# High and low parts of a short last row group side by side in one stationary block

## The chip, the cores and the metric

The kernel runs on one core of one Trainium2 chip. The metric is the time of one execution on the device in microseconds (us). The core has five engines that run at the same time and wait for each other through semaphores: TensorE (PE in the profile, its weight loads PEld), VectorE (DVE), ScalarE (ACT), GpSimd (POOL) and SyncE (SP), which here issues loads. Sixteen DMA engines move data.

## The reference

Windowed attention makes 8 x 544 = 4352 rows of 512 values. Each row goes to one of eight experts, and the expert's two layers are applied to it. Which expert a row gets is known only once the attention is done.

```
logits = einsum('bsd,de->bse', x, w_gate)
local_gate = 1 / (1 + exp(-einsum('bsd,de->bse', x, w_local)))
for b in range(8):
    for s in range(544):
        fresh = argmax(logits[b, s])
        e = fresh if s == 0 or local_gate[b, s] < 0.5 else prev_e
        prev_e = e
        p = softmax(logits[b, s])
        h = maximum(x[b, s] @ w1[e], 0)          # 512 -> 1024
        out[b, s] = p[e] * (h @ w2[e])           # 1024 -> 512
```

## The kernel before

The first third of the time is attention. Routing then makes, on the chip, lists of the rows of each expert. The rest is the expert part, class `Moe`, which works in blocks. An early block and a full block take 256 rows of an expert. Each expert also has one remainder block, called e0 to e7 below, which takes what is left over after its blocks of 256 and, where the expert has a block of 256 that no other block took, those 256 rows as well. Rows stand in groups of 128, numbered 0 to 3: in a remainder block with a block of 256, groups 0 and 1 are those 256 rows, and groups 2 and 3 the remainder.

Products are made to full precision from two roundings each: a value is the sum of a high part and a low part, and a product of two values is three products, high by high, high by low and low by high. The weights come in eight pieces of 512 KB for a block, four for each layer; `load` issues one on SyncE, `split` rounds it to its high part on ScalarE (L1150) and subtracts on VectorE for its low part (L1160).

A remainder block runs like this:

- `block` reads the case number of the expert, which routing wrote into `cnd`, and enters one of 34 copies of the code with `Switch`. Case 0 is `half`, a remainder of at most 128 rows with no block of 256. Case 2 and up are `part` with 256 rows and a remainder of 8, 16, ... 256 rows. All five engines jump into the case and out of it at its end.
- `mm1`, first layer: for each of eight slices `fc` of 128 hidden values, 12 products (L1251) with the weights stationary and the rows as columns, so the width of a product is the number of rows. ScalarE takes the positive part as high part into `HH` (L1253), VectorE the low part into `HL` (L1254). The eight slices rotate through five banks of PSUM, `ps` 2, 3, 6, 1, 7.
- `mm2`, second layer: for each row group, for each slice, three products of 128x512 (L1262) in which the rows' high or low parts are the stationary block of 128 x 128 and the weights' parts stream past. That is 24 products for a group, into one bank.
- `store` scales a group's result by each row's probability (ScalarE, L1267) and scatters the rows to the output (GpSimd, L1268).
- `xpose` transposes one row group of the next block on TensorE (L1205), and ScalarE and VectorE copy its parts (L1207, L1208). Groups 0 and 1 are transposed in the case, after 9 and 18 second-layer products; groups 2 and 3 in `close`.
- `close` stands behind the case and is the same code for all cases of an expert: it stores the group that the case left in `ps[7]`, makes the 24 products of group 2, works out the scales of the next block (`scals`, L1217 to L1219, the first VectorE work after a case) and gathers the rows of the block after it (`gather`, GpSimd, L1191).

In the order of row groups, a remainder over 128 ran `[3, 0, 1]` and then 2 in `close`; a smaller one `[0, 1]` and then 2.

Two generators do the routing in small steps, hidden behind the early blocks: `Moe.hook` runs after each slice of an early block and takes one step of them. `Route.lists` writes the numbers of the row groups that each block gathers into `cid`, compares them with each row's number, and multiplies one-hot tables on TensorE (L999, 34 products) to get the rows' indices; two of its steps are taken per hook. `kinds` makes the case numbers, three steps per hook, and `rest` the indices of all later blocks, two per hook. In the middle of the second layer of the last early block `finish` runs what is missing up to the case numbers, at once.

## Time and profile before

| | us |
|---|---|
| median of 3 runs | 699.48 |
| lowest and highest run | 695.32, 699.75 |
| the profiled execution, its time | 698.19 |
| the profiled execution, its span | 696.5 |

The span runs from the first to the last instruction of the profiled execution; 1.7 us lie around it. The mean granted clock of TensorE was 0.990. Attention ends near 240 us, the early blocks run to 326 us, the remainder blocks to 619 us, three full blocks to 688 us.

Lines of a timeline have the start in us, the duration of the run of instructions, the engine, the source line, the operation, its output and inputs by name, the shapes, and the number of instructions; in brackets, how long the engine was idle before it and what ended the wait. Durations of matmuls overlap, so the pace of a run is read from starts, or from the chain of waits, where a row has the start, the time that it adds to the chain, and the number of instructions.

### The profile page before, as it was taken

What the parts mean: (1) busy time and instruction counts of PE and PEld (TensorE: products, weight loads), DVE (VectorE), ACT (ScalarE), POOL (GpSimd) and SP (SyncE); (2) the same over time, 40 slices, a digit from 0 to 9 for tenths busy, and PEclk for the clock granted to TensorE, in tenths of its full rate; (3) what the DMA queues carried; (4) which work ended last, traced back from release to release, by engine and by line L of the source; (5) the groups of instructions that cost most, each with busy time, mean ns of one, the idle gap of its engine ahead of it and who ended that gap; (6) DMA issues with size and microseconds to landing.
All of it is one profiled execution on the core that took longest, in us unless ns stands there. A gap on an engine that the chain in (4) does not pass through costs nothing.

```text
span 696.5 us, 18391 instructions
## 1 busy us (share of the span) xinstructions
PE 671.7 (96%) x7253; PEld 564.2 (81%) x7253; DVE 427.4 (61%) x1057; ACT 342.6 (49%) x614; POOL 196.2 (28%) x321
## 2 busy tenths in 40 slices
PE   9999999999899899998997999999999999999995
PEld 7777777777677787897886898889898989888994
DVE  7878777678887777995516645426353516345563
ACT  4555555655454674652326535334444425255563
POOL 7634344243333301032013303031304021032033
PEclk9999999999999999999999999999999999999998
DMA  8956967866846497776517666428385417265673
GB/s 331 387 213 238 353 235 274 311 240 226 309 181 262 140 353 247 257 230 238 191 60 257 200 219 200 145 76 257 126 260 158 159 66 235 67 211 179 234 259 112
DMA packets 43014, 151.46 MB, mean 217 GB/s; under 512 B 7965, under 2 KB 9245, under 8 KB 38688
## 3 DMA queue, kind: packets, MB, share of 16 engines
q1 hardware_dynamic: 35536, 126.92, 51.5%
q0 software_dynamic: 6960, 21.90, 9.8%
q8 instruction: 77, 1.26, 0.7%
q14 instruction: 153, 1.25, 0.5%
q10 hardware_dynamic: 288, 0.13, 0.1%
HBM read 130.55 MB, written 19.69 MB: 216 GB/s over the span
## 4 chain that ended last, share of the span: by engine, by line
PE 59%; DVE 3%; issue 1%; ACT 1%; POOL 0%; DVEq 0%; ACTq 0%; POOLq 0%
PE ps L1262 28%; PE ps L1251 26%; PE ps L1205 3%; DVE wp L1160 1%; DVE wq L1160 1%; PE ps L1374 0%; DVE xT L991 0%; PE ps L999 0%; POOL xa L1191 0%; DVE xT L989 0%; DVE hl L1254 0%; DVE wp L1208 0%; PE ps L276 0%; PE ps L1363 0%; DVE xl L1160 0%
## 5 line engine op out<-in xcount | busy, mean ns | idle before, releaser
L1268 POOL DMA_INDIRECT out_dram<-y,tk x39 | 40.5, 1039 | 320.0 <-ACT y L1267 257.0
L1262 PE MATMUL ps<-wp,wq 128*128 128x512 f32 x504 | 128.0, 401 | 0.9 <-ACT wq L1365 0.9
L1262 PEld LDWEIGHTS ps<-wp,wq 128*128 128x128 f32 x504 | 93.2, 190 | 20.5 <-ACT wq L1365 1.1
L1251 PE MATMUL ps<-wp,wp 128*128 128x256 f32 (+6 forms) x672 | 107.8, 320 | 0.0
L1251 PEld LDWEIGHTS ps<-wp,wp 128*128 128x128 f32 x672 | 103.4, 189 | 3.6
L1254 DVE SCALAR_TENSOR_TENSOR wq<-ps,wq 128x256 fp32r<-128x256 f32 (+6 forms) x80 | 41.3, 519 | 71.8 <-ACT wq L1253 71.6
L191 POOL TENSOR_SCALAR_AFFINE_SELECT qbd<-raw 64x512 f32<-64x512 f32 x62 | 44.6, 719 | 119.5 <-PE ps L243 100.6
L1208 DVE TENSOR_TENSOR wp<-ps,wp 128x512 fp32r<-128x512 f32 x40 | 27.4, 690 | 80.0 <-ACT wp L1207 80.0
L1253 ACT ACTIVATE wq<-ps 128x256 fp32r<-128x256 f32 (+6 forms) x80 | 36.8, 463 | 77.3 <-PE ps L1251 69.6
L243 PE MATMUL ps<-kx,qbd 128*64 128x128 f32 x1024 | 71.4, 281 | 1.8 <-issue 1.7
L243 PEld LDWEIGHTS ps<-kx,qbd 128*64 128x64 f32 x1024 | 55.1, 137 | 12.7 <-issue 8.3
L1267 ACT ACTIVATE y<-ps,pp 128x512 f32<-128x512 f32 x39 | 26.9, 689 | 76.4 <-PE ps L1262 70.8
L248 DVE TENSOR_REDUCE mx<-ps 128x4 f32<-128x512 f32 x64 | 43.9, 686 | 29.3 <-PE ps L243 29.3
L1160 DVE TENSOR_TENSOR wp<-raw,wp 128x1024 fp32r<-128x1024 f32 x47 | 56.9, 1216 | 2.5 <-ACT wp L1150 2.5
L254 ACT ACTIVATE pe<-pe 128x512 f32<-128x512 f32 x64 | 40.7, 636 | 32.9 <-DVE pe L250 32.9
L1191 POOL DMA_INDIRECT xa<-xs,idx x42 | 51.3, 1220 | 17.1 <-issue 10.0
L1150 ACT CAST wp<-raw 128x1024 fp32r<-128x1024 f32 x49 | 50.7, 1045 | 1.3 <-DMA raw<-in_w_dram 0.5
L1207 ACT CAST wp<-ps 128x512 fp32r<-128x512 f32 x40 | 23.4, 588 | 55.4 <-PE ps L1205 55.4
L250 DVE TENSOR_TENSOR pe<-ps,mx 128x512 f32<-128x512 f32 x64 | 44.0, 688 | 1.6
L276 PE MATMUL ps<-v,pt 128*32 128x65 f32 x2048 | 42.7, 222 | 2.1 <-DVE xa L284 0.8
L276 PEld LDWEIGHTS ps<-v,pt 128*32 128x32 f32 x2048 | 33.3, 110 | 13.8 <-issue 6.7
L191 POOL TENSOR_SCALAR_AFFINE_SELECT kx<-raw 128x384 f32<-128x384 f32 (+3 forms) x127 | 42.7, 369 | 3.0 <-DMA raw<-in_qk_dram 0.9
(279 smaller groups left out, 1173.0 us busy)
## 6 DMA issues: line engine op xcount, KB each, us to landing
raw<-in_w_dram SPq DMA_DIRECT2D x78, 512.0 KB, 3.9
v<-in_vw_dram SPq DMA_DIRECT2D x32, 1040.0 KB, 9.9
raw<-in_qk_dram SPq DMA_DIRECT2D x32, 528.0 KB, 8.2
xa<-in_w_dram SPq DMA_DIRECT2D x26, 512.0 KB, 5.0
xT<-in_w_dram SPq DMA_DIRECT2D x20, 512.0 KB, 4.1
xs<-xa SPq DMA_DIRECT2D x8, 1056.0 KB
qgb<-in_qg_dram SPq DMA_DIRECT2D x8, 128.0 KB
xa<-xs,idx POOLq DMA_INDIRECT x42
```

The source lines that it names most:

```text
L191: self.nc.gpsimd.affine_select(out=out, in_=in_, pattern=pat, compare_op=ALU.is_ge, fill=0.0, base=0, channel_multiplier=0)
L243: nc.tensor.matmul(sp[64 * t2:64 * t2 + 64, t], qbd[:, w], kf[:, f:f + P], start=False, stop=True, skip_group_check=True)
L248: nc.vector.tensor_reduce(out=mx, in_=st["sp"], axis=AX.X, op=ALU.max)
L250: nc.vector.tensor_tensor(out=st["pe"][:, 4 * hb:4 * hb + 4], in0=st["sp"], in1=mx.broadcast_to([P, 4, P]), op=ALU.subtract)
L254: self.nc.scalar.activation(out=pe, in_=pe, func=AF.Exp, scale=SCALE)
L276: nc.tensor.matmul(o[32 * w4:32 * w4 + 32, g, h], pt[:, 2 * g + w4 // 2, w4 % 2, h, :], v[:, w, h * (D + 1):(h + 1) * (D + 1)], start=True ...
L1150: nc.scalar.copy(out=hi, in_=raw)
L1160: (nc.gpsimd if pool else nc.vector).tensor_tensor(out=lo, in0=raw, in1=hi.bitcast(F32), op=ALU.subtract)
L1191: self.nc.gpsimd.indirect_dma_start(out=self.xr[j] if k == "early" else self.xr4[:, j], out_offset=None, in_=src, in_offset=bass.IndirectO ...
L1251: nc.tensor.matmul(ph, a[:, dc, fs], b_[:, dc, n0:n1], start=(n == 0), stop=(n == 11))
L1254: nc.vector.scalar_tensor_tensor(out=hl[:, fc, n0:n1], in0=ph, scalar=0.0, in1=hh[:, fc, n0:n1].bitcast(F32), op0=ALU.max, op1=ALU.subtract)
L1262: nc.tensor.matmul(py, a[:, fc, js], b_[:, fs], start=(fc == 0 and k == 0), stop=(fc == 7 and k == 2))
```

## The change

In a remainder block whose last row group has at most 64 rows (`HALF`), the low parts of the first layer's values of that group are no longer written to `HL`. They go into `HH`, into the columns 64 to 127 of group 3, beside the high parts in columns 0 to 63. The second layer of that group, `thin`, then takes two products for a slice, the block by the weights' high part and by their low part, 16 in place of 24. In its result the partitions 0 to 63 hold what the high parts gave and 64 to 127 what the low parts gave (with low by low, which was left out before), for the same rows. `store` adds the two: ScalarE scales the lower half into `y`, VectorE scales the upper half and adds.

For this the last group is always group 3. With a remainder of at most 128 rows the block of 256 moves from groups 0 and 1 to 1 and 2, and the first layer reads columns 128 to 384 + `few` in place of 0 to 256 + `few`. Routing takes that into account: `lists` shifts the numbers of the row groups by one for such experts, with six small instructions in place of two and four yields more. The order of groups in the case is `[0, 3, 1]` over 128; up to 128 it is the first half of the slices of group 1, then group 3, then the second half of group 1. `close` is unchanged, and so is the number of gathers.

```diff
-        cr = cid[:, 0:2 * E].rearrange("p (e a) j -> p e a j", a=2)
+        cr = cid[:, 0:2 * E].rearrange("p (e a) j -> p e (a j)", a=2)
-        nc.vector.tensor_scalar(out=cr[:, :, 0, 0], in0=self.nbc, scalar1=-4.0, scalar2=None, op0=ALU.add)
-        yield
-        nc.vector.tensor_scalar(out=cr[:, :, 1, 0], in0=self.nbc, scalar1=-2.0, scalar2=None, op0=ALU.add)
+        rm = self.tmp("rm", [P, E], I32)
+        nc.vector.tensor_scalar(out=rm, in0=self.cn, scalar1=255, scalar2=None, op0=ALU.bitwise_and)
+        yield
+        sh = self.tmp("sh", [P, E], F32)
+        nc.vector.tensor_scalar(out=sh, in0=self.left, scalar1=0.0, scalar2=None, op0=ALU.is_ge)
+        yield
+        nc.vector.scalar_tensor_tensor(out=sh, in0=rm, scalar=float(P), in1=sh, op0=ALU.is_le, op1=ALU.mult)
+        yield
+        fb = self.tmp("fb", [P, E], F32)
+        nc.vector.scalar_tensor_tensor(out=fb, in0=self.nbc, scalar=-4.0, in1=sh, op0=ALU.add, op1=ALU.subtract)
+        yield
+        nc.vector.tensor_tensor(out=cr, in0=fb.rearrange("p (e o) -> p e o", o=1).broadcast_to([P, E, 4]),
+                                in1=self.io8[:, 0:4].rearrange("p (o j) -> p o j", o=1).broadcast_to([P, E, 4]), op=ALU.add)
+        yield
+        nc.vector.scalar_tensor_tensor(out=cr[:, :, 0], in0=sh, scalar=4.0, in1=fb, op0=ALU.mult, op1=ALU.add)
         yield
...
-        nc.vector.scalar_tensor_tensor(out=hl[:, fc, n0:n1], in0=ph, scalar=0.0, in1=hh[:, fc, n0:n1].bitcast(F32), op0=ALU.max, op1=ALU.subtract)
+        for o, a, b_ in [(hl, n0, n1)] if not few else [(hl, n0, n1 - few), (hh, n1 - few, n1)]:
+            c = a if o is hl else P * (NSL - 1) + HALF
+            nc.vector.scalar_tensor_tensor(out=o[:, fc, c:c + b_ - a], in0=ph[:, a - n0:b_ - n0], scalar=0.0, in1=hh[:, fc, a:b_].bitcast(F32), op0=ALU.max, op1=ALU.subtract)
...
+    def thin(self, i, py, fc, j, hh):
+        hi, lo = self.wp[8 * i + 4 + fc // 2]
+        fs = slice(512 * (fc % 2), 512 * (fc % 2) + 512)
+        for k, b_ in enumerate((hi, lo)):
+            self.nc.tensor.matmul(py, hh[:, fc, P * j:P * j + P], b_[:, fs], start=(fc == 0 and k == 0), stop=(fc == 7 and k == 1))
...
+        if thin:
+            nc.scalar.activation(out=y[rows], in_=py[HALF:P], func=AF.Copy, scale=g[HALF:P, js])
+            nc.vector.scalar_tensor_tensor(out=y[rows], in0=py[rows], scalar=g[rows, js], in1=y[rows], op0=ALU.mult, op1=ALU.add)
...
+        thin = 0 < few <= HALF
+        if thin:
+            g = self.g[0]
+            self.nc.vector.tensor_copy(g[HALF:P, 3:4], g[0:HALF, 3:4])
...
-            n = 256 + GRAIN * (case - 1)
-            self.part(i, 0, n, [3] * (n > 384) + [0, 1])
+            few = GRAIN * (case - 1)
+            if few <= P:
+                self.part(i, P, 384 + few, [(1, range(4)), (3, range(8)), (1, range(4, 8))], few)
+            else:
+                self.part(i, 0, 256 + few, [(0, range(8)), (3, range(8)), (1, range(8))], few - P)
```

On TensorE, in the case of e3 with 184 remainder rows (last group 56), this stood where the group in the middle of the three is worked out. A row is a source line, the operation, output and inputs with buffer numbers, the shape and a count; `ps_64` is the bank, `wq_4314` is `HH`, `wq_4315` is `HL`, the `wp` are pieces of weights. Before, group 0 stood there, of which these are the first half:

```order
L1262 MATMUL ps_64<-wp_101,wq_4314 128x512 x2
L1262 MATMUL ps_64<-wp_101,wq_4315 128x512
L1262 MATMUL ps_64<-wp_101,wq_4314 128x512 x2
L1262 MATMUL ps_64<-wp_101,wq_4315 128x512
L1262 MATMUL ps_64<-wp_4207,wq_4314 128x512 x2
L1262 MATMUL ps_64<-wp_4207,wq_4315 128x512
L1262 MATMUL ps_64<-wp_4207,wq_4314 128x512 x2
L1262 MATMUL ps_64<-wp_4207,wq_4315 128x512
```

After, in the same place, group 3, with the first rows of group 1 behind it:

```order
L1284 MATMUL ps_64<-wp_101,wq_4314 128x512 x4
L1284 MATMUL ps_64<-wp_4207,wq_4314 128x512 x4
L1284 MATMUL ps_64<-wp_4208,wq_4314 128x512 x4
L1284 MATMUL ps_64<-wp_4312,wq_4314 128x512 x4
L1278 MATMUL ps_70<-wp_101,wq_4314 128x512 x2
```

Group 3 moved from the front to the middle, reads only `HH`, and has 16 products.

On VectorE, in the routing behind the second early block, the two instructions that wrote `cid` stood here before (`nbc` counts groups, `wp` rows split a piece of weights):

```order
L1254 SCALAR_TENSOR_TENSOR hl<-ps_66,hh 128x256
L1011 TENSOR_SCALAR cid<-nbc 128x8
L1013 TENSOR_SCALAR cid<-nbc 128x8
L1017 TENSOR_TENSOR mf<-ge,sd 128x104
L1020 SCALAR_TENSOR_TENSOR k_4713<-ek,k_269 128x13
L1160 TENSOR_TENSOR wp_4311<-xa_108,wp_4311 128x1024
```

After, `rm` is the remainder, `sh` tells whether an expert's groups are shifted, `fb` is the first group's number:

```order
L1270 SCALAR_TENSOR_TENSOR hl<-ps_66,hh 128x256
L1014 TENSOR_SCALAR rm<-cn 128x8
L1017 TENSOR_SCALAR sh<-left 128x8
L1019 SCALAR_TENSOR_TENSOR sh<-rm,sh 128x8
L1022 SCALAR_TENSOR_TENSOR fb<-nbc,sh 128x8
L1174 TENSOR_TENSOR wp_4311<-xa_108,wp_4311 128x1024
L1024 TENSOR_TENSOR cid<-fb,io_262 128x32
L1027 SCALAR_TENSOR_TENSOR cid<-sh,fb 128x8
```

`mf` and all routing steps after it stand two hooks later than before.

On ScalarE, at the end of the case of e5 with 32 remainder rows, the copies of the next block's transposed groups 0 and 1 (`wp_4209`, from the banks 68 and 67) stood together, with the store of group 0 (`y_4318`, from bank 63) as the last work before the jump:

```order
L1253 ACTIVATE wq_4314<-ps_69 128x288
L1207 CAST wp_4209<-ps_68 128x4x128
L1207 CAST wp_4209<-ps_67 128x4x128
L1267 ACTIVATE y_4318<-ps_63,pp_94 128x512
L1566 UNCONDITIONAL_BRANCH
```

After:

```order
L1267 ACTIVATE wq_4314<-ps_69 128x288
L1221 CAST wp_4209<-ps_68 128x4x128
L1293 ACTIVATE y_4318<-ps_64,pp_94 64x512
L1221 CAST wp_4209<-ps_67 128x4x128
L1608 UNCONDITIONAL_BRANCH
```

The store is that of group 3, covers 64 partitions and comes ahead of the second copy. That copy now comes behind the sixth slice of group 1 and is the last work before the jump.

More of the change, by code (lines that the diff above doesn't have):

```diff
@@ L49 @@
 REM = 2
+NSL = 4
+HALF = P // 2
 NPIECE = 12
@@ L1393, in part @@
                 self.nc.gpsimd.drain()
[L1394 removed]
+            self.mm1(i, fc, *x, n0, n1, self.ps[(2, 3, 6, 1, 7, 2, 3, 6)[fc]], few if thin else 0)
             self.step(fc % 2 == 0, fc != 4)
[L1396 to L1407 removed]
+        last = work[-1][0]
+        banks = {}
+        k = 0
+        for j, fcs in work:
+            py = banks.setdefault(j, self.ps[7] if rem and j == last else self.py.t[len(banks)])
+            for fc in fcs:
+                if thin and j == 3:
+                    self.thin(i, py, fc, j, self.HH)
+                    continue
+                self.mm2(i, py, fc, j, *x[2:])
+                if k == 0:
+                    self.step(0, 1)
+                if k in (2, 5):
+                    self.xpose(i + 1, k // 3)
+                k += 1
+            if not (rem and j == last):
+                self.store(py, j, thin and j == 3)
     def close(self, i, j):
@@ L1462, in block @@
         else:
-            self.part(i, 0, 256, [0])
+            self.part(i, 0, 256, [(0, range(8))])
             self.close(i, 1)
```

35 lines of the change are left out of this document (14 added, 21 removed).

## The prediction

> **What bounds the kernel now.** I read the page's head and its chain of waits first, to see which engine holds the end; then TensorE's timeline, for the form of each expert block; then stretches by block, for the room the other engines have; and last the rows around the two places where the change adds work. "Block" with e0 to e7 is the remainder block of that expert; the three blocks after e7 have full groups alone and are not touched.
>
> ```profile
> span 696.5 us, 18391 instructions
> PE 671.7 (96%) x7253; PEld 564.2 (81%) x7253; DVE 427.4 (61%) x1057; ACT 342.6 (49%) x614; POOL 196.2 (28%) x321
> ...
> PE 59%; DVE 3%; issue 1%; ACT 1%; POOL 0%; DVEq 0%; ACTq 0%; POOLq 0%
> ```
>
> TensorE is busy in 96% of the span and leads the chain. Its share of the chain is smaller only because the chain is followed back part of the way. From 393 us on TensorE is never idle; three stretches, the first two of them blocks that the change shortens:
>
> ```profile
> core 0: us, PE busy (x) PEld busy (x) DVE busy (x) ACT busy (x) POOL busy (x), PEclk, DMA share, GB/s
> 426.60:469.70 43.10, 43.10 (x209) 37.62 (x209) 17.02 (x24) 16.74 (x25) 8.45 (x9) 1.00 0.45 146
> 503.40:534.60 31.20, 31.20 (x185) 27.81 (x184) 15.54 (x24) 14.78 (x24) 7.47 (x8) 1.00 0.62 198
> 619.00:642.60 23.60, 23.60 (x154) 21.34 (x153) 13.86 (x21) 13.14 (x20) 5.52 (x5) 1.00 0.66 224
> ```
>
> The second number of each row is the stretch, the third TensorE's busy time in it: the same. VectorE has work for 17.02 of 43.1 us in e3, ScalarE for 16.74. The last row is a full block. It needs the same eight weight pieces as e3, gets them in 23.6 us, and TensorE doesn't wait. So weights would not stop a shorter e3.
>
> The timeline shows which blocks the change shortens, since a first-layer product is as wide as the block has rows:
>
> ```profile
> 326.05 20.20 PE L1251 MATMUL ps<-wp,wp 128*128 128x456 f32 x96
> ...
> 393.01 4.00 PE L1251 MATMUL ps<-wp,hh 128*128 128x352 f32 x24
> ...
> 426.65 0.96 PE L1251 MATMUL ps<-wp,xh 128*128 128x440 f32 x4
> ...
> 469.74 3.85 PE L1251 MATMUL ps<-wp,wp 128*128 128x344 f32 x24
> ...
> 503.42 6.48 PE L1251 MATMUL ps<-wp,wp 128*128 128x288 f32 x48
> ...
> 534.63 14.56 PE L1251 MATMUL ps<-wp,wp 128*128 128x440 f32 x72
> ...
> 578.00 17.93 PE L1251 MATMUL ps<-wp,wp 128*128 128x408 f32 x96
> ```
>
> These are e0, e2, e3, e4, e5, e6, e7 (e1 runs another case). Width less 256 is the remainder, in steps of 8: 200, 96, 184, 88, 32, 184, 152. Over 128, the last group holds 128 less: 72, 96, 56, 88, 32, 56, 24. At most 64 rows: e3, e5, e6, e7. Four blocks become thin.
>
> **The change part by part.** *Removed products.* Each thin block loses 8 of 24 products of 128x512, 32 in all. Their pace stands in the chain, where such products run back to back:
>
> ```profile
> 451.07 14.50 PE ps L1262 x63
> ...
> 521.36 9.07 PE ps L1262 x39
> ...
> 559.09 14.69 PE ps L1262 x63
> ...
> 601.00 18.18 PE ps L1262 x78
> ```
>
> One row from each thin block: 14.50 + 9.07 + 14.69 + 18.18 = 56.44 us for 63 + 39 + 63 + 78 = 243 products, 0.2323 us each. The pace is what a removed product gives back, not its duration, which overlaps the next one's. 32 x 0.2323 = 7.43 us. The Trainium skill, "TensorE: Matmul & The Clock Gate", section on 56 against 53.3 ns, gives N / 2.4 GHz plus 2.5 ns, an estimate of 215.8 ns for 512 columns; by that the term would be 6.9 us. The rows are 16.5 ns slower per product, and the measurement decides.
>
> *First layer.* Same widths, shifted columns: nothing on TensorE. The subtraction on VectorE becomes two instructions per slice in thin blocks, 8 more short ones each. VectorE is idle for 26.1 of 43.1 us in e3, and first-layer results rotate through five banks: nothing. The low parts of the last slice are read by the last two products of a group, 14 or more products after the first layer ends; the last VectorE subtraction was needed by the third to last before, too. Were that cover gone, it would be one small instruction per slice, and the last rows of the routing fence below put such a one at 0.07 to 0.36 us.
>
> *Store of the thin group.* One ScalarE instruction over 64 partitions, one more on VectorE behind it, and a scatter of 64 rows. In e3, e6 and e7 a whole further group of 24 products (5.6 us) comes after it and hides it. In e2, e4 and e5 only 12 products (2.8 us) come behind the last group, which matters for the way out of the case, below.
>
> *Routing.* Six small VectorE instructions stand for two, and four more yields push all later routing work two hooks down. Here VectorE, not TensorE, ends the stage:
>
> ```profile
> 285.32 0.17 DVE L1011 TENSOR_SCALAR cid<-nbc 128x8 bf16<-128x8 f32 x1
> 285.39 0.17 DVE L1013 TENSOR_SCALAR cid<-nbc 128x8 bf16<-128x8 f32 x1
> ...
> 301.08 0.42 DVE L1254 SCALAR_TENSOR_TENSOR hl<-ps,hh 128x256 fp32r<-128x256 f32 x1 [0.33 <-ACT hh L1253]
> ...
> 303.87 0.42 DVE L1254 SCALAR_TENSOR_TENSOR hl<-ps,hh 128x256 fp32r<-128x256 f32 x1 [0.59 <-ACT hh L1253]
> ...
> 304.75 0.16 DVE L1052 TENSOR_SCALAR kq<-kq 1x8 int32<-1x8 int32 x1
> ...
> 306.99 0.42 DVE L1254 SCALAR_TENSOR_TENSOR hl<-ps,hh 128x256 fp32r<-128x256 f32 x1 [0.28 <-ACT hh L1253]
> ...
> 319.73 1.28 DVE L1208 TENSOR_TENSOR wp<-ps,wp 128x512 fp32r<-128x512 f32 x2
> ```
>
> ```profile
> 297.74 1.01 PE L999 MATMUL ps<-xT,o 128*128 128x8 bf16 x34
> ...
> 315.22 0.60 PE L1205 MATMUL ps<-idf,xa 128*128 128x128 f32 x4
> ...
> 320.46 0.97 PE L1205 MATMUL ps<-idf,xa 128*128 128x128 f32 x4 [2.10 <-DVE wp L1208]
> ```
>
> TensorE's transposes at 320.46 have waited 2.10 us for VectorE's L1208 of 319.73. From 285 to 320 VectorE is full but for waits of 0.33, 0.59 and 0.28 us. An independent small instruction costs 0.07 us there (285.32 to 285.39), a dependent one up to 0.36 (into 304.75). Three of the six hang on the one before: about 3 x 0.2 + 3 x 0.07 = 0.8, less 0.14 for the two removed, 0.7 us. Least: the three waits sum to 1.20 us and swallow it, 0. Most: 0.7, and five small instructions of the case numbers (0.7 us) that now come after the last wait, 1.4. Following the new order through those waits, I get VectorE at L1208 0.5 us later, and take 0.5. The 34 routing products at 297.74 move two slices down (2.9 us), and the first gathers with them:
>
> ```profile
> 305.03 1.83 POOL L1191 DMA_INDIRECT xa<-xs,idx  x1 [0.30 <-issue]
> ```
>
> The last gather leaves GpSimd at 306.86, now some 309.8, and the first transposes want rows at 315.22: hidden, with 5 us over. The order of SyncE's loads and of GpSimd's instructions is unchanged. TensorE waits for VectorE 2.10 us in any case, which also covers the wait of each queue for the later case number.
>
> *The way out of a case.* A case ends in a jump, and the next instruction of ScalarE or VectorE comes late:
>
> ```profile
> 384.03 0.37 ACT L1365 CAST wq<-ps 128x256 fp32r<-128x256 f32 x1 [0.81 <-PE ps L1363]
> 388.81 0.69 ACT L1267 ACTIVATE y<-ps,pp 128x512 f32<-128x512 f32 x1 [4.40 <-issue]
> ...
> 391.75 0.59 ACT L1207 CAST wp<-ps 128x512 fp32r<-128x512 f32 x1
> ```
>
> ```profile
> DVE tm L1217 <- issue: 24.4, 8, 3.6
> ```
>
> ```profile
> 451.11 0.59 ACT L1207 CAST wp<-ps 128x512 fp32r<-128x512 f32 x1 [1.93 <-PE ps L1205]
> 452.49 0.69 ACT L1267 ACTIVATE y<-ps,pp 128x512 f32<-128x512 f32 x1 [0.80 <-PE ps L1262]
> ```
>
> ```profile
> 450.82 14.74 PE L1262 MATMUL ps<-wp,wq 128*128 128x512 f32 x63
> ...
> 528.17 1.57 PE L1262 MATMUL ps<-hl,wq 128*128 128x512 f32 x6
> ```
>
> ScalarE stood 4.40 us in "issue" on leaving e1's case; VectorE, whose first work after each of the eight cases is L1217, 24.4 us in all, 3.05 each and 3.6 at most. TensorE's own jumps, as into 426.65, show no gap. The Trainium skill, "Runtime: NRT & Kernel Launch", Instruction fetch mechanics, says that a taken branch to a page that isn't loaded stalls until it is fetched; by that rule, which speaks against work near a case's end, ScalarE and VectorE agree and TensorE doesn't. Now e5: the transposed copy of its successor's second row group moves from the first group to two slices before the end. ScalarE's copy ends 0.88 us after TensorE goes on (450.82 to 451.11 + 0.59), and TensorE has 6 products left, 1.40 us. So ScalarE leaves 0.52 us before TensorE does, T. After the jump w, e1's rows need 3.53 us (388.81 to 392.34) to the last transposed copy that the next first layer reads: T - 0.52 + w + 3.53. TensorE gets there at T + 6.46 (528.17 to 534.63). With w = 3.05 nothing is lost, with 4.40 it is 0.95 us. I take 0.5. In e2 and e4 ScalarE's last work is the store of the last group. Such a store ends 0.97 us after the next group begins (452.49 + 0.69, against 450.82 + 6 x 0.2323), 12 products or 2.80 us are left, so it ends 1.83 before T and w may reach 4.74. So nothing, even at 4.40. e2 itself, which now reads the fourth row group as well, has its copy by 392.34 and starts at 393.01.
>
> *Sum.* 7.43 - 0.5 - 0.5 = 6.4 us. Against the profiled execution: 698.19 - 6.4 = 691.8. Against the median, 699.48, it is 693.1. The profiled execution lies 1.3 us under the median, and a repeat of either kernel can land on either side, so I put the time at the middle, 692.4. Bounds: costs from 0 to 1.4 + 0.95 leave a gain of 5.1 to 7.4.
>
> **The rivals.** *All of it.* The waits of VectorE swallow the routing work, and the jump takes 3.05: gain 7.43, 691.4 by the same middle (698.8). For it speak the 1.20 us of waits and the eight exits of VectorE near 3 us; against it that the three waits lie ahead of part of the work that was pushed down.
>
> *Little of it.* What TensorE saves comes back as a wait for something with less slack than I saw: the transposed rows or the low parts of a first slice. Price: half of the gain, 3.7 us, 695.1; all of it, 698.8. The stretches speak against it: full blocks run at 23.6 us with less room than thin ones would have.
>
> *Slower.* Leaving a case takes ScalarE longer, because VectorE's program has grown and cases lie elsewhere. It costs e5 w - 3.42 (6.46 - 3.53 + 0.52, less 0.03 for the signal) and e2 and e4 w - 4.74 each. It eats the gain of 6.9 where 3w = 19.9, so from w = 6.6 us; at w = 9 it is 5.6 + 2 x 4.3 = 14.2, less 6.9: 7.3 over the middle, 706.1. The longest seen is 4.40. The rule on taken branches named above is this mechanism.
>
> **How the numbers follow.** About 1% (7.0 us) is what a measurement of this kernel tells from no change; the three runs shown are 4.4 us apart. My case, gains of 5.1 to 7.0, has 0.60; all of it 0.22; little of it 0.15; slower than before 0.03. My case lies 0.6 us under the 1% line, so a repeat's scatter lifts it over in somewhat more than a third: 0.22. All of it goes over in 0.14 of its 0.22, and little of it in 0.01. Faster by over 1%: 0.37. Slower by over 1%: the one mechanism, 0.02. Within: 0.61. The range runs from 689.0, which is 7.4 under the middle and 2.4 of scatter more, to 697.0, which takes in the half of "little of it". Left out are some 0.07 of "all of it", 0.07 of "little of it" and the slower case.
>
> **What would show it.** Right: first-layer products unchanged in number; 32 second-layer products fewer; e3, e6, e7 each 1.9 us shorter with TensorE idle 0; e5 shorter by 1 to 1.9, with any gap right before e6's first product; the gap at about 320 us at 2.1 to 3.5. Wrong: a gap ahead of e3's, e5's or e7's last products, an idle row after e2 or e4, or a pace away from 0.232. If the products are gone but the blocks no shorter, then TensorE was not the bound there and my first step falls.

## The result, and the profile after

| | before | after |
|---|---|---|
| median of 7 runs, us | 698.98 | 690.93 |
| lowest and highest run | 694.94, 699.75 | 688.73, 692.57 |
| the profiled execution, its time | 698.19 | 688.73 |
| its span | 696.5 | 687.0 |

The ratio of the times is 0.9905, with a 95% interval of 0.9882 to 0.9928: a gain of 6.6 us by the ratio, 5.0 to 8.2 by its interval, and 8.05 by the two medians. The 692.4 us of the prediction are 1.5 us above the measured median, which lies in the range from 689.0 to 697.0. The parts of the sum did less well than the sum: the products came out to the hundredth, but one term was 2 us too low, and a gain of 1.4 to 2.5 us was not in it at all.

The head of the page after, and the shares of its chain of waits:

```profile
span 687.0 us, 18390 instructions
...
PE 661.7 (96%) x7221; PEld 556.2 (81%) x7221; DVE 432.9 (63%) x1101; ACT 342.6 (50%) x614; POOL 196.5 (29%) x321
...
PE 56%; DVE 6%; issue 1%; ACT 1%; POOL 0%; DVEq 0%; POOLq 0%; ACTq 0%
```

TensorE is busy for 10.0 us less and has 32 matmul records fewer (7253 to 7221), as many as products were taken out. Of the 10.0 us, 7.3 fall in the blocks from e2 to e7, where those products stood. VectorE, 3% of the chain before, is 6% of it now. That is the first sign that something in VectorE's hands came onto the path.

The chain of waits after, from e3 to the first full block. A row has the start, the time that it adds to the chain, the engine, the output's name, the line, and the number of instructions. L1265 is the first layer (before: L1251), L1278 a full product of the second layer (L1262), L1284 one of the two-part products:

```profile
425.43 19.21 PE ps L1265 x96
...
451.09 3.73 PE ps L1284 x16
...
466.85 15.26 PE ps L1265 x96
...
500.71 12.74 PE ps L1265 x96
...
516.68 3.73 PE ps L1284 x16
...
530.08 19.22 PE ps L1265 x96
...
555.74 3.70 PE ps L1284 x16
...
571.42 17.77 PE ps L1265 x96
...
595.61 3.69 PE ps L1284 x16
...
610.30 11.41 PE ps L1265 x96
```

The four runs of two-part products take 3.73 + 3.73 + 3.70 + 3.69 = 14.85 us for 64, or 0.2320 each, the pace of the products before. The starts of the first layers give the blocks' lengths. From e3 to e7 they are 41.42, 33.86, 29.37, 41.34 and 38.88 us; before, by the same reading, 43.1, 33.7, 31.2, 43.4 and 41.0. TensorE does not wait in the thin ones, as the stretches of e3 and e5 show:

```profile
core 0: us, PE busy (x) PEld busy (x) DVE busy (x) ACT busy (x) POOL busy (x), PEclk, DMA share, GB/s
425.27:466.69 41.42, 41.42 (x202) 36.12 (x200) 18.45 (x34) 16.75 (x25) 9.23 (x10) 1.00 0.48 158
500.55:529.92 29.37, 29.37 (x178) 26.34 (x176) 15.63 (x33) 13.85 (x23) 6.63 (x7) 1.00 0.58 198
```

Busy time again equals the stretch, and VectorE's 17.02 us in e3 became 18.45 with ten more instructions, without anybody waiting for it.

TensorE around the routing stage, where the prediction had put a cost of 0.5 us. L1001 is the index products (before: L999, at 297.74):

```profile
299.29 1.22 PE L1265 MATMUL ps<-xh,wp 128*128 128x256 f32 x8 [1.68 <-DVE hl L1270]
...
300.83 1.01 PE L1001 MATMUL ps<-xT,o 128*128 128x8 bf16 x34
...
311.09 0.72 PE L1278 MATMUL ps<-wq,hh 128*128 128x512 f32 x2 [0.64 <-ACT wp L1164]
...
321.36 0.66 PE L1219 MATMUL ps<-idf,xa 128*128 128x128 f32 x4 [2.23 <-DVE wp L1222]
```

The wait at 321 us that was there before (2.10 us) is 2.23 us now, so nothing seems to have happened there. But two waits stand ahead of it that the prediction didn't have: 1.68 us for VectorE's subtraction at 299.29, and 0.64 us at 311.09. At the first place, before, TensorE and VectorE had this:

```profile
300.22 1.22 PE L1251 MATMUL ps<-xh,wp 128*128 128x256 f32 x8
...
299.75 0.74 DVE L1254 SCALAR_TENSOR_TENSOR hl<-ps,hh 128x256 fp32r<-128x256 f32 x2
```

In an early block the slices rotate through three banks, so the fourth slice of the first layer takes the PSUM bank of the first, which VectorE's first subtraction (299.75 and on) sets free. Before, TensorE came to the fourth slice at 300.22, because the 34 index products had kept it busy from 297.74 on, and it found the bank free. Now the index products come behind that point, and TensorE stands with nothing to do in front of the bank.

Put together by stages, this is where the 9.5 us between the two spans come from:

| stage | before | after | difference |
|---|---|---|---|
| up to the first early product | 233.46 | 231.84 | -1.62 |
| early blocks and routing, up to e0 | 92.59 | 95.12 | +2.53 |
| e0 and e1 | 66.96 | 64.47 | -2.49 |
| thin blocks e3, e5, e6, e7 | 158.69 | 151.01 | -7.68 |
| e2 and e4 | 67.32 | 67.70 | +0.38 |
| three full blocks and the end | 77.48 | 76.86 | -0.62 |

The first row is not the change's: attention is the same code, and other executions of these two kernels reach that point anywhere from 231.7 to 234.1 us. The second row is five times the 0.5 us that the prediction took, and the third it didn't have.

### The profile page after: what moved, and what is told of

Its sections match the earlier page's. It is cut to its first block, busy times and chain, and to the rows that moved or that the text cites. A ratio compares the mean times of both kernels' runs of the same rounds, so it can differ in the third digit from the quotient of the medians.

```text
span 687.0 us, 18390 instructions
## 1 busy us (share of the span) xinstructions
PE 661.7 (96%) x7221; PEld 556.2 (81%) x7221; DVE 432.9 (63%) x1101; ACT 342.6 (50%) x614; POOL 196.5 (29%) x321
## 4 chain that ended last, share of the span: by engine, by line
PE 56%; DVE 6%; issue 1%; ACT 1%; POOL 0%; DVEq 0%; POOLq 0%; ACTq 0%
PE ps L1265 26%; PE ps L1278 23%; PE ps L1219 2%; PE ps L1284 2%; DVE wp L1174 1%; DVE wq L1174 1%; PE ps L1001 0%; DVE xT L993 0%; DVE xT L991 0%; DVE xl L1174 0%; ACT wp L1164 0%; DVE wp L1222 0%; POOL xa L1205 0%; DVE o L907 0%; DVE xl L1222 0%
## 5 line engine op out<-in xcount | busy, mean ns | idle before, releaser
L1297 POOL DMA_INDIRECT out_dram<-y,tk x39 | 40.8, 1047 | 310.6 <-ACT y L1296 231.7
L1278 PE MATMUL ps<-wp,wq 128*128 128x512 f32 x444 | 114.2, 402 | 0.9 <-ACT wq L1394 0.9
L1265 PE MATMUL ps<-wp,wp 128*128 128x256 f32 (+6 forms) x672 | 107.7, 320 | 0.0
L1265 PEld LDWEIGHTS ps<-wp,wp 128*128 128x128 f32 x672 | 103.5, 188 | 3.5
L1278 PEld LDWEIGHTS ps<-wp,wq 128*128 128x128 f32 x444 | 82.0, 190 | 17.9 <-ACT wq L1394 1.1
L1270 DVE SCALAR_TENSOR_TENSOR wq<-ps,wq 128x384 fp32r<-128x384 f32 (+4 forms) x112 | 43.1, 412 | 56.8 <-ACT wq L1267 47.2
L1296 ACT ACTIVATE y<-ps,pp 128x512 f32<-128x512 f32 x35 | 24.2, 690 | 61.6 <-PE ps L1278 49.0
L278 PEld LDWEIGHTS ps<-v,pt 128*32 128x32 f32 x2048 | 33.4, 110 | 13.6 <-issue 8.0
```

The lines of the kernel that those rows point to most:

```text
L278: nc.tensor.matmul(o[32 * w4:32 * w4 + 32, g, h], pt[:, 2 * g + w4 // 2, w4 % 2, h, :], v[:, w, h * (D + 1):(h + 1) * (D + 1)], start=True ...
L1265: nc.tensor.matmul(ph, a[:, dc, fs], b_[:, dc, n0:n1], start=(n == 0), stop=(n == 11))
L1270: nc.vector.scalar_tensor_tensor(out=o[:, fc, c:c + b_ - a], in0=ph[:, a - n0:b_ - n0], scalar=0.0, in1=hh[:, fc, a:b_].bitcast(F32), op0= ...
L1278: nc.tensor.matmul(py, a[:, fc, js], b_[:, fs], start=(fc == 0 and k == 0), stop=(fc == 7 and k == 2))
L1297: sc = nc.gpsimd.indirect_dma_start(out=self.out, out_offset=bass.IndirectOffsetOnAxis(ap=tk[rows, js], axis=0), in_=y[rows], in_offset=No ...
```

## The experiments

Twelve more runs were made; three of them (c_after, c_before and c_pool) repeat a program that another run has. In this table "third early block" is cut in three by TensorE's rows: its first layer, its second layer up to the last routing products, and the rest up to e0's first product; the clock is the granted one in the middle piece. "e0 and e1" runs from e0's first product to e2's first; "e1's case" from the case's first product to the first product of its `close`. Ratios are to the kernel before on the same chip, whose medians there were 694.19 for c_after to e_pool, 694.76 for c_before to a_fill and 694.04 for a_fillv to c_pool.

| kernel | median us | ratio, 95% interval | third early block | clock | e0 and e1 | e1's case |
|---|---|---|---|---|---|---|
| before, of the result | 698.98 | | 12.65, 16.88, 1.66 | 0.90 | 66.96 | 14.77 |
| after, of the result | 690.93 | 0.9905 (0.9882 to 0.9928) | 14.39, 17.21, 2.21 | 0.93 | 64.47 | 12.12 |
| c_after | 689.32 | 0.9927 (0.9901 to 0.9953) | 14.37, 16.14, 2.30 | 1.00 | 64.82 | 12.03 |
| e_nothin | 697.05 | 1.0042 (1.0018 to 1.0067) | 14.39, 16.13, 2.35 | 1.00 | 66.60 | 14.65 |
| e_yields | 686.8 | 0.9889 (0.9848 to 0.9931) | 13.53, 14.97, 2.88 | 1.00 | 65.80 | 12.62 |
| e_pool | 684.23 | 0.9852 (0.9802 to 0.9901) | 12.54, 14.97, 2.84 | 1.00 | 62.71 | 10.76 |
| c_before | 694.0, one run | | 12.65, 14.98, 2.65 | 1.00 | 66.24 | 15.46 |
| b_yields | 697.34 | 1.0041 (1.0016 to 1.0065) | 13.94, 17.32, 2.10 | 0.93 | 65.50 | 14.38 |
| b_order | 695.73 | 1.0020 (0.9998 to 1.0041) | 12.66, 14.98, 2.58 | 1.00 | 65.67 | 13.28 |
| a_fill | 687.8 | 0.9893 (0.9854 to 0.9932) | 14.39, 17.68, 1.71 | 0.91 | 63.08 | 10.77 |
| a_fillv | 690.82, one run | | 14.36, 17.20, 2.22 | 0.93 | 63.67 | 10.76 |
| a_filla | 689.04, one run | | 14.35, 16.14, 2.72 | 1.00 | 65.39 | 12.62 |
| b_fill | 692.71 | 0.9978 (0.9953 to 1.0002) | 12.67, 14.98, 3.01 | 1.00 | 62.92 | 10.60 |
| c_pool | 682.99 | 0.9843 (0.9822 to 0.9864) | 12.53, 16.58, 1.73 | 0.90 | 62.50 | 10.76 |

My theory ahead of the first four: the 32 products give their 7.4 us; the routing stage costs what the two traces show, through the later hooks and the added instructions; and what e0 and e1 won is something else. The rivals are named with the expectations.

### The changed kernel again (c_after)

> The changed kernel as it is, as the measure for the others and to see which stretches repeat. If the 66.96 to 64.47 us of e0 and e1 belong to the program (where its code lies or in which order it runs), they come out within 0.3 us of 64.5 again, and the stretch from the first product of the first early block to e0's first product within 0.3 us of 95.1. If they are chance of one execution, e0 and e1 fall anywhere from 64 to 67, and the 1.6 us by which attention ended earlier need not repeat.

It gave 0.9927, with an interval that overlaps the first one's. From e2 on its blocks repeat those of the result within 0.02 us. e0 and e1 repeat to 0.35 us, just outside the 0.3 expected, and e1's case to 0.09: most of what shortened e1's case belongs to the program and not to one execution. The stretch up to e0 did not repeat: it is 93.36 us in place of 95.1, of which 0.8 are in the first early block (37.73 in the result, 36.94 here). The middle piece of the third early block differs by 1.07 us at a clock of 0.93 against 1.00, so the routing stage has to be compared at equal clocks.

### All row groups with 24 products (e_nothin)

```diff
-        thin = 0 < few <= HALF
+        thin = False
```

> Group 3 runs with 24 products again; its place, the row numbers and the routing stay as in the changed kernel. Theory: the saving is the 32 products alone, so e3, e5, e6, e7 come back to 43.1, 31.2, 43.3, 41.0 us within 0.3, +1.9 us each, and the kernel is 7.4 us slower than the changed one (7 to 8). Rival: part of the saving came from the new order of groups; then less than 5 us come back and the four blocks stay under those lengths.

TensorE's timeline of this kernel; each row is the first one of a block's first layer, of e3, e4, e5 and e6 (widths 440, 344, 288, 440):

```profile
427.09 0.97 PE L1265 MATMUL ps<-wp,xh 128*128 128x440 f32 x4
...
470.38 3.98 PE L1265 MATMUL ps<-wp,wp 128*128 128x344 f32 x24
...
504.24 6.54 PE L1265 MATMUL ps<-wp,wp 128*128 128x288 f32 x48
...
535.49 14.59 PE L1265 MATMUL ps<-wp,wp 128*128 128x440 f32 x72
```

e3 takes 470.38 - 427.09 = 43.29 us and e5 31.25, against 41.42 and 29.37 with the two-part products. The four blocks together give 1.87 + 1.88 + 1.86 + 1.83 = 7.44 us. This is the first term of the sum, apart from the order, the shifted columns and the routing: 7.43 was predicted. The rest of the change, without its products, is slower than before by 0.18 to 0.67%.

This also shows what is not the reason that e3 won only 1.67 us between the profiles and e7 2.13: in this kernel e3 is 0.20 longer than before, e6 0.17 and e7 0.31 shorter. These shifts of 0.2 to 0.3 us are there without two-part products.

### Two hooks fewer (e_yields)

Of the six small instructions all stay on VectorE, but with the two yields of before.

```diff
         nc.vector.tensor_scalar(out=rm, in0=self.cn, scalar1=255, scalar2=None, op0=ALU.bitwise_and)
-        yield
...
         nc.vector.tensor_scalar(out=sh, in0=self.left, scalar1=0.0, scalar2=None, op0=ALU.is_ge)
-        yield
...
         nc.vector.scalar_tensor_tensor(out=fb, in0=self.nbc, scalar=-4.0, in1=sh, op0=ALU.add, op1=ALU.subtract)
-        yield
...
-        yield
         nc.vector.scalar_tensor_tensor(out=cr[:, :, 0], in0=sh, scalar=4.0, in1=fb, op0=ALU.mult, op1=ALU.add)
```

> The six routing instructions stay, but with two yields in place of six, so later routing work stands at the hooks where it stood before. Theory (what cost 2.5 us in the routing is that the 34 index products and the case numbers moved two hooks down, out of waits that hid them): from the first early product to e0 93.2 us in place of 95.1 (93.0 to 93.6), 1.9 us faster than the changed kernel. Rival (the six instructions themselves lengthen the chain): 94.7 to 95.1, 0 to 0.4 us faster.

The index products stand ahead of the fourth slice again, and TensorE's wait for the bank, 1.67 us in c_after, becomes

```profile
300.57 1.22 PE L1261 MATMUL ps<-xh,wp 128*128 128x256 f32 x8 [0.81 <-DVE hl L1266]
```

0.81 us. The second layer is back at 14.97 us. The third early block is 31.38 us long against 32.81 in c_after, both at a granted clock of 1.00: the later hooks cost 1.43 us. The stretch up to e0 is 91.89 us, 1.47 less than in c_after. That is under the 1.9 expected and well over the 0.4 of the rival: both causes are there, and the hooks are the larger one. The 93.2 itself was missed, since it was counted down from 95.1, which did not repeat.

### The six instructions on GpSimd (e_pool, and c_pool for an interval)

The same values, worked out in twelve small GpSimd instructions with two yields; VectorE keeps none of them.

```diff
-        nc.vector.tensor_scalar(out=rm, in0=self.cn, scalar1=255, scalar2=None, op0=ALU.bitwise_and)
...
+        gp = nc.gpsimd
+        gp.tensor_copy(rm, self.tmp("f2", [P, E], I32))
+        gp.tensor_copy(fb, self.cn)
+        gp.tensor_scalar(out=rm, in0=rm, scalar1=-128.0, scalar2=None, op0=ALU.mult)
+        gp.tensor_tensor(out=rm, in0=rm, in1=fb, op=ALU.add)
...
-        nc.vector.scalar_tensor_tensor(out=cr[:, :, 0], in0=sh, scalar=4.0, in1=fb, op0=ALU.mult, op1=ALU.add)
+        gp.tensor_scalar(out=sh, in0=sh, scalar1=4.0, scalar2=None, op0=ALU.mult)
+        gp.tensor_tensor(out=cr[:, :, 0], in0=sh, in1=fb, op=ALU.add)
```

> As with two yields, and the six small instructions run on GpSimd (as twelve there), off VectorE. Theory: VectorE has less to do than before the change, so the stretch to e0 is 92.6 us or up to 0.3 less, 2.5 us faster than the changed kernel. Rival (the list of groups comes late from GpSimd, with instructions of 0.3 us and more in a row, and the comparison that needs it waits): VectorE shows a wait on GpSimd ahead of its first comparison, and the stretch is 93.2 or longer.

The third early block takes 30.35 us, against 31.38 in e_yields and 30.28 in the kernel before at the same clock (c_before). So the instructions had cost another 1.0 us on VectorE and cost nothing on GpSimd; the wait for the bank is gone. The stretch up to e0 is 90.87 us, 2.49 less than in c_after, as expected (2.5), and VectorE shows no wait for GpSimd there, so the rival falls.

> The changed kernel with its six routing instructions on GpSimd and two yields, again, for an interval: 0.983 to 0.987 of the time before, by -7.4 for the products, 0 for routing and -3 to -4 for e0 with e1. If the first result was chance: 0.990 to 0.993, as the changed kernel.

0.9843, with 0.9822 to 0.9864: faster than the kernel before, and faster than the changed one, whose interval doesn't overlap. It is the best version found. About 2.5 us of what it wins over the changed kernel is routing. Another 2.3 us are e0 and e1 (62.5 against 64.8), and those are not earned by routing, as the next sections show: TensorE is idle in e1 for nearly as long in the two traces (3.95 and 4.06 us), but in c_after 6.8 us of e1 ran at half clock, and none in c_pool.

### The kernel before again (c_before)

> The kernel before, unchanged, for a second trace of it. Theory (the lengths of blocks belong to the program, not to one execution): e0 with e1 66.9 to 67.0 us, e1's case 14.8 long with ScalarE's first copy there some 4 us late and VectorE's on time, the thin candidates e3, e5, e6, e7 at 43.1, 31.2, 43.4, 41.0, the first layer of the third early block at 12.65, and no TensorE wait at 300 us. The stretch from the first early product to e0's first product: the trace of before had 92.6, with 37.8 in the first early block; on the chip of the other runs that block took 36.9, so 91.0 to 91.8 here. Rival (chance): e1's case differs by more than 1 us from 14.8.

The stretches of the first and the second layer of the third early block, with TensorE's, its weight loads', VectorE's, ScalarE's and GpSimd's busy time, the granted clock, the DMA share and the rate. First this kernel:

```profile
292.29:304.94 12.65, 12.65 (x131) 12.46 (x130) 11.49 (x31) 6.19 (x11) 5.89 (x5) 1.00 0.68 225
304.94:319.92 14.98, 13.19 (x67) 10.35 (x65) 13.67 (x21) 7.12 (x10) 1.02 (x1) 1.00 0.68 233
```

and the changed one (c_after):

```profile
294.69:309.06 14.37, 12.70 (x131) 12.45 (x130) 11.46 (x25) 6.20 (x11) 6.63 (x5) 1.00 0.62 199
309.06:325.20 16.14, 13.25 (x67) 10.25 (x65) 14.69 (x27) 7.22 (x10) 1.25 (x1) 1.00 0.69 228
```

At a clock of 1.00 in both, the first layer is 1.72 us longer and the second 1.16, the rest 0.35 shorter: 32.81 - 30.28 = +2.53 us for the routing stage. In the first layer TensorE has the same work (12.65 and 12.70 us), and the difference is the wait for the bank. In the second, VectorE has 1.02 us more work there (13.67 to 14.69), pushed down from above. The result's own pair, at 0.90 and 0.93, gives 33.81 - 31.19 = +2.62. e1's case came out at 15.46, 0.7 longer than in the other trace of this program, within the expected 1 us; e0 with e1 at 66.24, under the 66.9 to 67.0 expected; the stretch up to e0 at 90.88, a little under the 91.0 to 91.8 expected.

### The four yields alone in the kernel before (b_yields)

```diff
         nc.vector.tensor_scalar(out=cr[:, :, 1, 0], in0=self.nbc, scalar1=-2.0, scalar2=None, op0=ALU.add)
         yield
+        yield from lag(4)
```

> The kernel before with the four additional yields alone and none of the new instructions. Theory A (moving the later steps two hooks down costs by itself, because the 34 index products come out from under the wait for the PSUM bank and because the case-number steps come behind VectorE's last wait): the first layer of the third early block 13.4 to 13.6 in place of 12.65, and the stretch up to e0 longer by 1.0 to 1.9 us than in the kernel before on the same chip. Rival B (only the added instructions cost): both unchanged within 0.2. The time by A 695 to 696, by B 694.2. The rest of the blocks as in before.

Not one instruction of arithmetic was added, and TensorE waits for the bank:

```profile
298.45 1.22 PE L1252 MATMUL ps<-xh,wp 128*128 128x256 f32 x8 [1.21 <-DVE hl L1255]
```

The first layer takes 13.94 us, over the 13.4 to 13.6 expected. The block is 33.36 us long at a clock of 0.93, against 31.19 at 0.90 in the kernel before: 2.17 us, more than the 1.0 to 1.9 expected. Against c_before, on the same chip, it is 3.08, but that trace ran at 1.00, so the 2.17 is the better measure. The time is 0.41% longer, 1.1 to 4.5 us by the interval; 697.3 us is outside the 695 to 696 expected. The rival, that only the instructions cost, falls. The two causes do not add up: yields alone 2.17, instructions alone 1.10 (e_yields against c_before), both 2.53 to 2.62. They push the same VectorE work past the same waits.

### The order of row groups alone (b_order)

```diff
-            self.part(i, 0, n, [3] * (n > 384) + [0, 1])
+            self.part(i, 0, n, [0] + [3] * (n > 384) + [1])
```

> The kernel before with the order of the changed kernel in blocks over 128 rows alone (group 0, group 3, group 1 in place of 3, 0, 1), all with 24 products for a group. Theory: no product is gained, the blocks stay as in before within 0.2 (e3 perhaps 0.2 longer, as with the two-part block switched off), and e1's case stays near 14.8, so e0 with e1 stays at 66.6 to 67.0. Rival: the order of groups is what made e0 with e1 2.5 us shorter in the changed kernel; then they come out at 64.5 here. Time by the theory within 0.3% of before, by the rival 2.5 us less.

All blocks from e2 on are those of c_before within 0.05 us, e3 included (43.09): the order as such is worth nothing. e0 and e1 came out at 65.67, between my 66.6 to 67.0 and the rival's 64.5, so both numbers were missed. e0 is 44.05 us long here as before. What moved is e1's case. ScalarE came 3.63 us late into it in place of 4.0 to 4.5, but that is the smaller part. First the case in c_before, then here:

```profile
366.62:382.08 15.46, 9.79 (x65) 8.89 (x64) 9.13 (x14) 8.61 (x16) 3.42 (x2) 0.89 0.84 282
```

```profile
368.74:382.02 13.28, 8.25 (x65) 7.34 (x64) 9.08 (x14) 8.31 (x16) 3.42 (x2) 1.00 0.94 308
```

The same 65 matmuls kept TensorE busy for 9.79 us at a mean clock of 0.89 and for 8.25 at 1.00. So 1.54 of the 2.18 us go with the granted clock, and 0.64 are waits.

### Code that isn't run (a_fill, a_fillv, a_filla, b_fill)

What e0 and e1 won lies at the jump into e1's case (`half`). These are ScalarE's first copy and VectorE's first instruction in that case, in the two kernels of the result; first before:

```profile
375.31 0.38 ACT L1377 ACTIVATE gsb<-ps 128x256 f32<-128x256 f32 x1 [4.03 <-issue]
...
371.73 0.06 DVE L1358 MEMSET tk<- 128x1 int32 x1
```

then after:

```profile
373.99 0.38 ACT L1406 ACTIVATE gsb<-ps 128x256 f32<-128x256 f32 x1 [2.21 <-PE ps L1403]
...
375.04 0.06 DVE L1387 MEMSET tk<- 128x1 int32 x1 [2.75 <-issue]
```

Before, VectorE was in the case at 371.73 and ScalarE came 4.03 us late, with no wait that the profile shows ("issue"). After, VectorE is the late one, by 2.75. ScalarE comes 3.40 us after the case's first product, against 5.20 before and 1.70 in c_after, where it is on time; so here it is still 1.7 us late, though its wait is put down to TensorE. Yet the change leaves the code of `half` as it was. To see whether the position of the code is what counts, these four kernels hold small instructions in one case of e0 that these inputs never enter (256 remainder rows; e0 has 200). Nothing more is executed.

```diff
+        if i == NX and case == NCASE - 1:
+            t = self.g[0][:, 3:4]
+            for _ in range(128):
+                self.nc.scalar.copy(out=t, in_=t)
+            for _ in range(128):
+                self.nc.vector.tensor_copy(t, t)
```

With both loops in the changed kernel (a_fill):

> The changed kernel with 128 small instructions on ScalarE and as many on VectorE in one case of e0 that these inputs do not enter: nothing more is executed, but the code behind it stands elsewhere. Theory (which engine comes late into e1's case depends on where its code stands): the first copy of ScalarE or VectorE's first instruction in e1's case changes its lateness by over 1 us, or another case's entry or exit does, and e1's case leaves 12.0 to 12.1 us. Rival (lateness follows from what the engines do before the jump): e1's case 12.0 to 12.2, VectorE 2.5 to 2.8 late and ScalarE on time as in the changed kernel, all blocks within 0.1 of it.

With VectorE's alone (a_fillv):

> The changed kernel with the 128 unexecuted instructions on VectorE alone. Theory (the lateness of an engine at a jump goes with the position of its own code): VectorE's first instruction in e1's case is on time in place of 2.6 to 2.8 us late, it is 4.3 to 4.6 late on leaving that case in place of 3.1 to 3.2, e1's case is 10.7 to 10.8 us; ScalarE as in the changed kernel. Rival (the ScalarE filler did it, or chance): e1's case 12.0 to 12.2, VectorE 2.6 late.

The same two rows of a_fillv:

```profile
375.23 0.39 ACT L1406 ACTIVATE gsb<-ps 128x256 f32<-128x256 f32 x1 [0.51 <-PE ps L1403]
...
375.18 0.06 DVE L1387 MEMSET tk<- 128x1 int32 x1
```

With ScalarE's alone (a_filla):

> The changed kernel with the 128 unexecuted instructions on ScalarE alone. Theory as for VectorE's: VectorE as in the changed kernel (2.5 to 2.8 us late into e1's case, 3.1 to 3.2 out of it), e1's case 12.0 to 12.2 us, ScalarE's entry on time. Rival: e1's case 10.7 to 10.8 us as with both fillers.

And of a_filla:

```profile
371.65 0.39 ACT L1406 ACTIVATE gsb<-ps 128x256 f32<-128x256 f32 x1 [0.50 <-PE ps L1403]
...
374.82 0.06 DVE L1387 MEMSET tk<- 128x1 int32 x1 [3.15 <-issue]
```

With both in the kernel before (b_fill):

> The kernel before with both fillers of 128 unexecuted instructions. Theory (the 1.4 to 2.5 us that e0 with e1 lost in the changed kernel belong to positions in the code, not to the change): the lateness of ScalarE (4.0 to 4.5 us) or of VectorE (on time) into e1's case, or on leaving it, moves by over 1 us, and e0 with e1 leaves 66.2 to 67.0 us by more than 0.5 to either side; nothing else moves by over 0.2. Rival (the old program's ScalarE is late there whatever stands ahead): e0 with e1 66.2 to 67.0, ScalarE 4.0 to 4.5 late.

And of b_fill:

```profile
369.02 0.38 ACT L1377 ACTIVATE gsb<-ps 128x256 f32<-128x256 f32 x1 [0.53 <-PE ps L1374]
...
368.95 0.06 DVE L1358 MEMSET tk<- 128x1 int32 x1
```

VectorE's filler alone brings VectorE into the case on time and makes it 10.76 us long, as both fillers do (10.77), and the exit is 4.21 us late, near the 4.3 to 4.6 expected; ScalarE's alone leaves VectorE late, and by a little more than expected (3.15 us; case 12.62). In the kernel before, both fillers bring ScalarE on time: the case takes 10.60 us in place of 15.46, and e0 with e1 62.92 in place of 66.24, 3.3 us less, for instructions that are not run. Of that the time shows less, 0.22% with an interval that just reaches no change, and the spans of the two traces differ by 2.9 us. In the third early block b_fill is 0.38 us longer than c_before, nearly all of it in "issue" ahead of e0, over the 0.2 expected. Each filler has one trace; where a program has two, the late engine's wait in "issue" repeats to 0.5 us (4.03 and 4.50, 2.75 and 2.56). So lateness at this jump follows where the code of the engines stands, and the old kernel can be rid of it as well.

That does not make all of the 1.4 to 2.5 us of e0 and e1 a matter of code position. These are what `close` of e1 took, from its first product to e2's, in two traces of the same program, before and c_before:

```profile
384.88:393.01 8.13, 8.13 (x32) 6.51 (x33) 3.59 (x7) 4.21 (x6) 2.63 (x3) 0.79 0.45 137
```

```profile
382.08:388.81 6.73, 6.71 (x33) 5.25 (x33) 2.59 (x6) 3.20 (x5) 1.93 (x2) 1.00 0.34 123
```

The clock was 0.79 in one and 1.00 in the other, and that is worth 1.4 us. In 12 of the 14 traces TensorE ran at half clock for some 3.4 or 6.8 us of e1, in a_fill and c_pool not at all. So the difference has three parts. e0, up to e1's first product, is 0.40 to 0.42 us shorter, in every kernel with the change's code (43.63 to 43.67), e_nothin included, than in those without it (44.04 to 44.07). TensorE's idle time in e1 is 1.14 us shorter in the result's pair (5.19 to 4.05) and 1.62 in c_before and c_after (5.68 to 4.06). The rest is TensorE's busy time in e1, at changing clocks: 0.93 less in the first pair, 0.61 more in the second. The idle time, 1.1 to 1.6 us, is what late engines cost directly, and that part is put down to where the code stands. Whether the half clock, which comes behind such waits in some executions, is theirs as well, these traces don't tell. In b_fill the idle time is 2.56 us against 5.68 in c_before, which is 3.1 of the 3.3 us won there.

On the way out of the same case it goes the other way, for VectorE. a_fill leaves e1's case with VectorE 4.53 us late, against 3.23 in the profile after and 3.09 in c_after. ScalarE is 5.55 us late there, and was so in those two as well (5.50 and 5.30). e2's first layer waits:

```profile
391.46 4.09 PE L1265 MATMUL ps<-wp,hh 128*128 128x352 f32 x24 [1.50 <-ACT wp L1221]
```

1.50 us, of which the changed kernel had 0.41 at that place (391.43). In a_fillv, with nearly the same lateness (5.37 and 4.21), it doesn't wait, but 6.0 us of that `close` ran at half clock, so TensorE came later itself.

## Why the prediction was right, and where it wasn't

*Removed products: right.* 32 x 0.2323 = 7.43 us; e_nothin against c_after isolates 7.44. The pace taken from the chain was the right price: the two-part products run at 0.2320. The estimate of 6.9 us from the Trainium skill, "TensorE: Matmul & The Clock Gate", section on 56 against 53.3 ns, would have been 0.5 us short.

*First layer and store: right.* The two subtractions per slice and the store of 64 rows cost nothing that shows: TensorE is busy without a gap from e2 to the end of e7.

*Routing: the step that failed.* The prediction took 0.5 us, from 0 to 1.4; it was 2.53 at equal clock. The arithmetic alone came near: 0.7 us of work was expected, and e_yields against c_before puts it at 1.10. What failed was the sentence that the 34 routing products "move two slices down (2.9 us)" and that this is hidden, "with 5 us over". That was true of the gathers which follow them. It wasn't asked what the products themselves had been hiding. Standing at 297.74, they were 0.87 us of work that TensorE did while VectorE freed the bank for the fourth slice, and so half of the 1.72 us that the first layer lost; the other half is VectorE's subtraction, late by the added instructions (0.81 us of wait in e_yields). Moved behind that point, they leave a wait in their old place and are paid for in the new one. b_yields shows it with no arithmetic at all: a wait of 1.21 us at this place. The rest, 1.16 us, comes in the second layer, where VectorE has a microsecond more to do: a wait of 0.68 us that wasn't there (0.64 in the result, at 311.09), and 0.42 more of the wait ahead of the transposes (1.79 us in c_before, 2.21 in c_after). "TensorE waits for VectorE 2.10 us in any case" was no cover either: that wait is where VectorE's lateness ends, not slack, and it did not shrink while everything ahead of it moved down.

*The way out of e5's case: the mechanism right, the size too high.* The copy of the second row group is ScalarE's last work ahead of the jump, as worked out. ScalarE there, and TensorE on the way into e6:

```profile
522.27 0.59 ACT L1221 CAST wp<-ps 128x512 fp32r<-128x512 f32 x1 [1.14 <-PE ps L1219]
525.82 0.69 ACT L1296 ACTIVATE y<-ps,pp 128x512 f32<-128x512 f32 x1 [2.96 <-issue]
...
528.77 0.59 ACT L1221 CAST wp<-ps 128x512 fp32r<-128x512 f32 x1
...
527.74 2.34 PE L1278 MATMUL ps<-wp,wq 128*128 128x512 f32 x9
529.92 2.37 PE L1265 MATMUL ps<-wp,wp 128*128 128x440 f32 x11
```

The jump w, bounded by 3.05 and 4.40, was 2.96. The last copy ends at 529.36 and e6 starts at 529.92 without a gap. So the term was 0 where 0.5 was taken, as it said of w = 3.05. The rule of the Trainium skill, "Runtime: NRT & Kernel Launch", Instruction fetch mechanics, that a taken branch to a page that isn't loaded stalls, agrees with the traces here, in which ScalarE or VectorE came 2.3 to 5.8 us late at jumps. That the fillers change the cost agrees with it too; which page of code was loaded when, no run here shows.

*Not in the prediction: e0 and e1, -1.4 to -2.5 us.* The prediction read the late ScalarE at e1's exit as a property of jumps, and looked at exits only. The entry of e1's case had 4.03 us of the same kind, on the path (TensorE waited there for ScalarE's copy), and it changed with the program. Of the gain, 1.1 to 1.6 us are that lateness, 0.4 are a shorter e0 whose cause is open, and the granted clock in e1 gave 0.9 in one pair of traces and took 0.6 in the other. Nothing in the profile of before could have said in which direction the lateness would go. That it could move at all by 2 to 3 us should have been in the range.

*The sum.* -7.68 of the thin blocks (7.44 of products, 0.24 of shifts that are left open), +2.53 and -1.4 to -2.5 give -6.6 to -7.6; +0.4 of e2 and e4 and -0.6 of the full blocks leave -6.8 to -7.9, where the ratio of the times has -6.6. The prediction had -6.4: one term was 2.0 us too kind, one 0.5 too harsh, and one of -1.4 to -2.5 was missing. That they nearly cancel is chance; the range was wide enough for any one of them, not because it knew them.

*The rivals.* "All of it" fails on the routing stage; "little of it" on the thin blocks, which have no wait. "Slower" named a real mechanism at the wrong place: at the exits of e2, e4 and e5, where it would have cost, ScalarE stood 3.06, 3.00 and 2.96 us after the change. The longest that it stood at any exit is 5.84 us, in b_fill on leaving e1's case, under the 6.6 from which the change would have lost.

*Left open.* Why e2, e3 and e4 are 0.2 us longer and e0, e6, e7 and the full blocks up to 0.4 shorter in the changed kernel, also with two-part products off. It is the pace of the same products: behind its first layer e7 takes 23.25 us in c_before and 22.94 in e_nothin for 104 matmuls each. In blocks over 128 rows the order of groups isn't it (b_order); the order of e2 and e4, their shifted columns and positions in memory weren't tried apart.

## What to carry to other kernels

When work is moved, ask of it two things: what hides it in its new place, and what it was hiding in the old one; work that an engine does ahead of a wait costs nothing as long as it is shorter than that wait. A wait that stands at the end of a chain of late work is no cover for more work on that chain. In a kernel with many jumps, a difference in a block that the change doesn't touch may come from where the code stands; unexecuted filler helps to tell it from a gain, and the granted clock of that block has to be looked at first.

## What wasn't expected of the hardware

Fourteen traces of eleven programs, with nothing changed in e1's case, showed ScalarE or VectorE from on time to 4.5 us late into it, and the case from 10.6 to 15.5 us long. 128 unexecuted instructions on VectorE alone turned its lateness off there, and at the exit its lateness went up (3.09 us in c_after, 4.21 in a_fillv). ScalarE's alone did not do that: VectorE stayed late (3.15 us in a_filla).

The granted clock in the second layer of the third early block was 1.00 in eight executions and 0.90 to 0.93 in six, with kernels of both kinds in each group, among them the same program (before 0.90, c_before 1.00). Stretches of the kernel before, ahead of the wait of 2.10 us for VectorE and from its end on; the granted clock stands third from the end:

```profile
314.00:318.30 4.30, 4.30 (x23) 3.25 (x22) 4.20 (x7) 1.19 (x3) 1.24 (x1) 1.00 0.55 202
...
320.70:324.00 3.30, 3.30 (x13) 2.81 (x12) 1.00 (x2) 0.99 (x2) 0.00 (x0) 0.50 0.65 264
...
324.40:326.00 1.60, 1.60 (x35) 1.60 (x34) 0.83 (x4) 0.69 (x1) 0.40 (x1) 1.00 0.18 38
```

From 0.2 us after the wait on, the clock is 0.50 for some 3.4 us, and four transposes take 0.97 us that take 0.66 in c_before, after a wait of 1.79 us and at a clock of 1.00. The Trainium skill, "TensorE: Matmul & The Clock Gate", Part 1, puts the fall to half clock behind an idle window of about 3.4 us that runs freely; that the fall comes in some executions of a program and not in others agrees, and that waits of 2.0 to 2.3 us were enough is shorter than it says. The second layer took 16.88 us in before and 14.98 in c_before, but the block as a whole only 31.19 and 30.28, since the fast one then stood 0.86 us in "issue" ahead of e0. A difference of a microsecond between two single traces can be that alone.
